# A new order inside each attention round: sums first, normalisation last, weight decoding from the fourth pair on

## The chip, the cores and the metric

The kernel runs on one core of one Trainium2 chip. The metric is the device time of one execution in microseconds (us); the time of a kernel is the median of its runs. Five engines work side by side, each through its own instruction stream in program order: PE (TensorE, matrix products; PEld is its loading of weights), DVE (VectorE), ACT (ScalarE), POOL (GpSimd) and SP (SyncE, which here only issues DMAs). They wait for one another through semaphores.

## The reference

Attention over 2 x 12 heads of 448 tokens and head size 64, with capped scores, then two gated layers. All arrays are float32 but the layers' weights, which arrive as float64.

```python
scores = cap * np.tanh(scale * (q @ k.T) / cap)
attn = np.exp(scores - max) ; attn = attn / (attn.sum(-1) + 1e-9)
x = (attn @ v)                                  # gathered to 896 tokens x 768
x = (silu(x @ w_gate) * (x @ w_val)) @ w_out    # 768 -> 1536 -> 768
x = (sigmoid(x @ w_gate2) * (x @ w_val2)) @ w_out2
```

## The kernel before, in words

Heads are handled in 12 pairs (b, p), two heads a pair, one pair a round of the loop over `i`. A float32 operand of a product is split into a high and a low part (`kh`, `kl`, `qh`, `ql`, `xh`, `xl`, `wh`, `wl`), and three products are summed. The schedule is written out by hand: each engine follows the order in which the program issues.

Keys come in three full blocks (c = 0 to 2) and a fourth, `NB`, in which both heads share a block. Round `i` does for pair `i`: `scores(i, c)` (PE into a two-bank PSUM tile `pss`, of which there are two, then a tanh on ACT into `e`), and `exponentials(i, part)` (exp on ACT, part 0 over blocks 0 and 1, part 1 over the rest). `sums(i, 0)` and `sums(i, 1)` (DVE) add the exponentials over blocks into `es`. One round later, `values(i - 1)` (PE) makes the numerators `pv` from `e` and `v` (16 products) and then the denominators `pd` from `es` and `e` (8 products). `taken_off` copies `pv` to `xu` and `pd` to `dn` and sends a row of `dn` for each head through a DMA into `g`. `inverted` takes the reciprocal of `g` (DVE), writes it to a DRAM tile `d`, and reads it back broadcast over partitions into `rb`. `normalized` multiplies `xu` by `rb` and splits the result into `xh` and `xl`, three operations on DVE.

`transposed(i + 2)` turns the next keys and queries on PE, and `qk_parts(i + 2)` splits them (four operations on DVE). `load` issues four DMAs a pair for k and q, `load_v` three for v. In the rounds, all DMAs are issued by SP, in program order: those of `load(i + 3)` and `load_v(i + 2)`, then `d` and two of `rb` in `inverted(i - 2)`, then `g` in `taken_off(i - 1)`.

`ws` is the stream of weights. A job loads 128 columns of a weight as 64-bit words (`r`, two buffers) and decodes them in four steps: L74 (DVE) and L75 (ACT); L77 and L78 (DVE); L80 (DVE) and L81 (ACT); L83 and L84 (DVE). A job that ends also issues the load of the job after next. Sixteen steps (four jobs) lie inside the attention, so that the first layer's products can start when the attention ends. After the rounds a written-out tail mixes the first products of the layer with the last pairs' values and normalisation; then the two gated layers run.

PSUM tiles of one bank (`pk`, `pq`, `pv`, `pd`) rotate through four buffers.

The edited functions and the loop follow, with the profile's line numbers.

Of the kernel before, what the change touches and what calls it, by code (L numbers as in the profile page):

```python
# [9 lines left out]
F32 = mybir.dt.float32  # L10
# [9 lines left out]
def attention_then_two_gated_layers(  # L20
# [14 lines left out]
    nc = tc.nc  # L35
    B, H, S, D = q.shape
    NT, DM = out.shape
    DFF = g1.shape[1]
    P = 128
# [3 lines left out]
    KD = DM // P  # L43
# [14 lines left out]
    xh = const.tile([P, KD, NT], F32R, tag="xh", name="xh")  # L58
    xl = const.tile([P, KD, NT], F32R, tag="xl", name="xl")
# [33 lines left out]
    class Stream:  # L93
# [11 lines left out]
        def load(self, upto):  # L105
            while self.loaded < min(upto, len(self.keys)):
                key = self.keys[self.loaded]
                src = self.jobs[key][0]
                r = wp.tile([P, src.shape[0] // P, src.shape[1]], I64, tag="r", name="r", bufs=2)
                nc.sync.dma_start(r, src.rearrange("(k p) f -> p k f", p=P))  # L110
                self.raw[key] = r
                self.loaded += 1
# [37 lines left out]
    def products(o, w, bh, bl, u, ks, nk, off=0):  # L150

        for kk in ks:
            for m, (a, x) in enumerate(((w[0], bh), (w[0], bl), (w[1], bh))):
                nc.tensor.matmul(  # L154
                    o,
                    lhsT=a[:, kk - off, :],
                    rhs=x[:, kk, halves[u]],
                    start=(kk == 0 and m == 0),
                    stop=(kk == nk - 1 and m == 2),
                )  # L160
# [133 lines left out]
    NPAIR = len(pairs)  # L294
    NB = S // P
    S0 = NB * P
    ws, pools, z_tiles = weights()
    with ExitStack() as actx:
        ap = actx.enter_context(tc.tile_pool(name="ap", bufs=2))
# [61 lines left out]
        def qk_parts(i, copy=nc.scalar.copy):  # L361

            pk, pq = turned.pop(i)
            kh, kl = [ap.tile([P, S0 + P], F32R, tag=n, name=n, bufs=2) for n in ("kh", "kl")]
            qh, ql = [ap.tile([P, S], F32R, tag=n, name=n, bufs=2) for n in ("qh", "ql")]
            nc.vector.tensor_copy(kh, pk)
            copy(qh, pq)
            nc.vector.tensor_tensor(kl, pk, kh.bitcast(F32), ALU.subtract)
            nc.vector.tensor_tensor(ql, pq, qh.bitcast(F32), ALU.subtract)
            operands[i] = (kh, kl, qh, ql)  # L370
# [3 lines left out]
        def scores(i, c):  # L374

            kh, kl, qh, ql = operands[i] if c < NB else operands.pop(i)
            if c == 0:
                ex[i] = ap.tile([P, 2 * NB + 1, S], F32, tag="e", name="e", bufs=2)
            keys = slice(c * P, (c + 1) * P)
            bank = bank2("pss")  # L380
            heads = rows if c < NB else [slice(0, P)]
            for t, (a, x) in enumerate(((kh, qh), (kl, qh), (kh, ql))):
                for j, r in enumerate(heads):
                    nc.tensor.matmul(bank[:, j, :S], lhsT=a[r, keys], rhs=x[r], start=(t == 0), stop=(t == 2))
            nc.scalar.activation(  # L385
                ex[i][:, 2 * c : 2 * c + len(heads)], bank[:, : len(heads), :S], AF.Tanh, scale=inv_sb
            )
# [7 lines left out]
        def sums(i, part):  # L395

            e = ex[i]
            if part == 0:
                es[i] = ap.tile([P, 2, S], F32, tag="es", name="es", bufs=2)
                nc.vector.tensor_tensor(es[i], e[:, 0:2], e[:, 2:4], ALU.add)  # L400
            else:
                nc.vector.tensor_tensor(es[i], es[i], e[:, 4:6], ALU.add)
# [3 lines left out]
        def values(i):  # L406

            e, tv, s = ex.pop(i), vt[i % NV], es.pop(i)
            pv, pd = bank1("pv"), bank1("pd")
            for c in range(NB + 1):  # L410
                for j in range(2):
                    y = e[:, 2 * c + (j if c < NB else 0)]
                    nc.tensor.matmul(pv[rows[j], :S], lhsT=tv[:, j, c, :], rhs=y, start=(c == 0), stop=(c == NB))
            for a, y in ((ones, s), (own, e[:, 2 * NB :])):
                for j in range(2):
                    nc.tensor.matmul(
                        pd[rows[j], :S], lhsT=a[:, j], rhs=y[:, j % y.shape[1]], start=(a is ones), stop=(a is own)
                    )
            nd[i] = (pv[:, :S], pd[:, :S])

        xu = {}
# [2 lines left out]

        def taken_off(i):
            n, d = nd.pop(i)
            xu[i] = ap.tile([P, S], F32, tag="xu", name="xu", bufs=3)
            dn = ap.tile([P, S], F32, tag="dn", name="dn", bufs=2)
            nc.scalar.copy(xu[i], n)
            nc.scalar.copy(dn, d)  # L430
            g = ap.tile([CP, 2 * R], F32, tag="g", name="g")
            nc.sync.dma_start(g, dn[0 : D + 1 : D])
            dens[i] = g

        def inverted(i):
            g = dens.pop(i)
            nc.vector.reciprocal(g, g)
            d = dr.tile([2 * S], F32, tag="d", name="d")
            nc.sync.dma_start(d.rearrange("(p c) -> p c", p=CP), g)
            rb[i] = ap.tile([P, S], F32, tag="rb", name="rb", bufs=2)  # L440
            for j in range(2):
                nc.sync.dma_start(rb[i][rows[j]], d[j * S : (j + 1) * S].unsqueeze(0).to_broadcast([D, S]))
# [7 lines left out]
        def normalized(i):  # L450
            b, p = pairs[i]
            x = ap.tile([P, S], F32, tag="x", name="x", bufs=2)
            nc.vector.tensor_tensor(x, xu.pop(i), rb.pop(i), ALU.mult)
            o = slice(b * S, (b + 1) * S)
            nc.vector.tensor_copy(xh[:, p, o], x)
            nc.vector.tensor_tensor(xl[:, p, o], x, xh[:, p, o].bitcast(F32), ALU.subtract)

        load(0, (nc.sync, nc.scalar))
        cap_sb = const.tile([P, 1], F32, name="cap_sb")
        nc.scalar.dma_start(cap_sb, cap.to_broadcast([P, 1]))  # L460
        wide_sb = const.tile([1, 1], mybir.dt.int32, name="wide_sb")
        inv_sb = fix.tile([P, 1], F32, name="inv_sb")
        near_sb = const.tile([P, 1], F32, name="near_sb")
        load(1)
        load_v(0)
        transposed(0)
        qk_parts(0)
        nc.vector.tensor_tensor(inv_sb, cap_sb, cap_sb, ALU.mult)
        nc.vector.tensor_scalar(wide_sb, inv_sb[:1], WIDEST**2, None, ALU.is_gt)
        nc.vector.tensor_scalar(near_sb, cap_sb, -WIDEST, WIDEST, ALU.max, ALU.min)  # L470
        nc.vector.reciprocal(inv_sb, near_sb)
        nc.vector.tensor_scalar_mul(inv_sb, inv_sb, scale)
        load(2)
        load_v(1)
        NS = 16
        for i in range(NPAIR):
            if i + 3 < NPAIR:
                load(i + 3)
            if i + 2 < NPAIR:
                load_v(i + 2)  # L480
            if i == 1:
                ws.load(2)
            if i > 1:
                inverted(i - 2)
            scores(i, 0)
            if i == 0:
                transposed(1)
                qk_parts(1, nc.vector.tensor_copy)
            scores(i, 1)
            exponentials(i, 0)  # L490
            if i > 0:
                sums(i - 1, 1)
                values(i - 1)
                taken_off(i - 1)
            for _ in range(NS * i // NPAIR, NS * (i + 1) // NPAIR):
                ws.step()
            sums(i, 0)
            scores(i, 2)
            scores(i, NB)
            exponentials(i, 1)  # L500
            if i + 2 < NPAIR:
                transposed(i + 2)
                qk_parts(i + 2, nc.vector.tensor_copy)
            if i > 1:
                normalized(i - 2)
        last = NPAIR - 1
        inverted(last - 1)
        sums(last, 1)
        ws.through(("v", 0, 0))
        begun = {0: (gate_banks(), value_banks())}  # L510
        w0 = [ws.take("g", 0, 0), ws.take("v", 0, 0)]
        products(begun[0][0][0], w0[0], xh, xl, 0, range(KD), KD)
        values(last)
        products(begun[0][1][0], w0[1], xh, xl, 0, range(KD), KD)
        normalized(last - 1)
        inverted_here(last)
        normalized(last)
        ws.through(("v", 0, 1))
        for o, w in zip(begun[0], w0):
            products(o[1], w, xh, xl, 1, range(KD - 1), KD)  # L520
        begun[1] = (gate_banks(), value_banks(), ws.take("g", 0, 1), ws.take("v", 0, 1))
        products(begun[1][0][0], begun[1][2], xh, xl, 0, range(KD), KD)
        for o, w in zip(begun[0], w0):
            products(o[1], w, xh, xl, 1, [KD - 1], KD)
    wide = nc.values_load(wide_sb[0:1, 0:1], min_val=0, max_val=1, skip_runtime_bounds_check_because="the result of a comparison")
    gated_layers(ws, pools, z_tiles, xh, xl, begun)

# [5 lines left out]
    with tc.If(wide != 0):  # L533
        xh = const.tile([P, KD, NT], F32R, tag="xh", name="xh_any")
# [95 lines left out]
```

## Time and profile before

| what | value |
|---|---|
| median of 3 runs | 667.99 us (666.84 to 668.14) |
| the profiled execution | 667.57 us |
| its span, first to last instruction | 665.8 us |
| PE, DVE, ACT busy | 96%, 68%, 42% of the span |
| values(0) starts | 26.35 us |
| values(10) starts | 117.35 us |
| layers' products start | 124.36 us |

The profile is of one execution. Times in its rows count from the span's first instruction; between the span and the time of the execution lie 1.8 us that no row shows. In the prediction V is the start of `values(i - 1)` in round i, and it serves as the mark of a round. The attention fills the first fifth of the span, and the gated layers the rest.

### The profile page before, as it was taken

The page shows a single profiled execution, that of the slowest core. Times are in us where ns is not written, and L with a number is a line of the kernel's source. Part 1 is how long each engine was busy: PE and PEld are TensorE (multiplying, and loading weights), DVE is VectorE, ACT ScalarE, POOL GpSimd, SP SyncE. Part 2 cuts the span into 40 slices and gives each one's busy share as a digit, 9 for nine tenths or more (in the row PEclk, how much of TensorE's full clock was granted, in tenths as well). Part 3 has the DMA queues.
Part 4 walks back from the last instruction along what each step waited for, and adds up shares of the span by engine and source line. Part 5 has one row for each costly group of instructions (what it writes and reads, how often), then busy time and mean ns, then how long its engine had stood idle before and what let it go on. Part 6 is the DMA issues. An engine that isn't in the chain of part 4 may idle for free. (4 is left out here: it accounts for less than half of the span.)

```text
span 665.8 us, 8385 instructions
## 1 busy us (share of the span) xinstructions
PE 642.1 (96%) x3311; PEld 546.6 (82%) x3311; DVE 453.6 (68%) x667; ACT 281.0 (42%) x363; POOL 3.3 (1%) x24
## 2 busy tenths in 40 slices
PE   6598999999999999999999999999999999999996
PEld 3354544499999999999999999999999999999995
DVE  3487787638879777997778667777787774694000
ACT  3598888604434433443334334334343332342000
POOL 2000000000000000000000000000000000000000
PEclk9699999999999999999999999999999999999998
DMA  5553542203434433433353423333443233161111
GB/s 140 148 146 94 137 115 85 76 1 95 138 100 142 143 96 95 143 114 123 117 168 100 139 95 95 114 124 103 135 137 101 95 98 94 58 206 43 41 29 33
DMA packets 99973, 70.86 MB, mean 106 GB/s; under 512 B 29142, under 2 KB 99926, under 8 KB 99926
## 3 DMA queue, kind: packets, MB, share of 16 engines
q1 hardware_dynamic: 98662, 69.80, 34.7%
q8 instruction: 28, 0.46, 0.3%
q10 hardware_dynamic: 1264, 0.45, 0.3%
q14 instruction: 19, 0.16, 0.1%
HBM read 67.40 MB, written 2.79 MB: 105 GB/s over the span
## 5 line engine op out<-in xcount | busy, mean ns | idle before, releaser
L75 ACT ACTIVATE c<-t,bias_sb 128x768 uint32<-128x768 uint32 x72 | 67.7, 940 | 94.3 <-DVE t L74 94.3
L81 ACT CAST wh<-c 128x768 fp32r<-128x768 f32 x60 | 50.4, 839 | 75.6 <-DVE c L80 75.6
L78 DVE SCALAR_TENSOR_TENSOR g<-r,g 128x768 f32<-128x768 uint32 x72 | 69.1, 959 | 2.5
L80 DVE SCALAR_TENSOR_TENSOR c<-r,c 128x768 uint32<-128x768 uint32 x72 | 68.5, 952 | 0.2 <-ACT c L75 0.2
L227 DVE TENSOR_TENSOR sg<-pv,sg 128x448 f32<-128x448 f32 x48 | 29.8, 620 | 51.0 <-PE pv L154 40.8
L84 DVE SCALAR_TENSOR_TENSOR wl<-g,t 128x768 fp32r<-128x768 f32 x60 | 57.5, 958 | 2.1
L228 ACT CAST hh<-sg 128x448 fp32r<-128x448 f32 x48 | 27.2, 567 | 73.6 <-DVE sg L227 73.6
L154 PE MATMUL pg<-xh,wh 128*128 128x448 f32 x144 | 52.8, 367 | 0.7 <-ACT e L385 0.7
L154 PE MATMUL pg<-hl,wh 128*128 128x448 f32 x144 | 53.0, 368 | 0.0
L154 PE MATMUL pg<-hh,wl 128*128 128x448 f32 x144 | 53.0, 368 | 0.0
L154 PE MATMUL pg<-hh,wh 128*128 128x448 f32 x144 | 53.0, 368 | 0.0
L154 PE MATMUL pv<-xh,wh 128*128 128x448 f32 x144 | 52.8, 367 | 0.0
L154 PE MATMUL pv<-yh,wl 128*128 128x448 f32 x144 | 52.7, 366 | 0.0
L154 PE MATMUL pg<-xl,wh 128*128 128x448 f32 x144 | 52.7, 366 | 0.0
L154 PE MATMUL pg<-yh,wh 128*128 128x448 f32 x144 | 52.7, 366 | 0.0
L154 PE MATMUL pg<-yl,wh 128*128 128x448 f32 x144 | 52.7, 366 | 0.0
L154 PE MATMUL pv<-xh,wl 128*128 128x448 f32 x144 | 52.7, 366 | 0.0
L154 PE MATMUL pg<-xh,wl 128*128 128x448 f32 x144 | 52.7, 366 | 0.0
L154 PE MATMUL pg<-yh,wl 128*128 128x448 f32 x144 | 52.7, 366 | 0.0
L154 PE MATMUL pv<-yl,wh 128*128 128x448 f32 x144 | 52.7, 366 | 0.0
L154 PE MATMUL pv<-xl,wh 128*128 128x448 f32 x144 | 52.7, 366 | 0.0
L154 PE MATMUL pv<-yh,wh 128*128 128x448 f32 x144 | 52.7, 366 | 0.0
(97 smaller groups left out, 1268.9 us busy)
## 6 DMA issues: line engine op xcount, KB each, us to landing
r<-in_moe_w_gate_dram SPq DMA_DIRECT2D x24, 768.0 KB, 4.3
r<-in_moe_w_val_dram SPq DMA_DIRECT2D x24, 768.0 KB, 4.5
r<-in_moe_w_out_dram SPq DMA_DIRECT2D x24, 768.0 KB, 4.1
tq<-in_q_dram SPq DMA_DIRECT2D x11, 224.0 KB, 3.9
rb<-d SPq DMA_DIRECT2D x22, 112.0 KB, 2.8
kt<-in_k_dram SPq DMA_DIRECT2D x12, 192.0 KB
vt<-in_v_dram SPq DMA_DIRECT2D x12, 192.0 KB, 3.3
out_dram<-ob SPq DMA_DIRECT2D x4, 140.0 KB
```

The costliest lines, as they stand in the source:

```text
L75: nc.scalar.activation(c, t, AF.Relu, bias=bias_sb, scale=4096.0)
L78: nc.vector.scalar_tensor_tensor(g, low, 2.0**-32, g.bitcast(U32), ALU.mult, ALU.add)
L80: nc.vector.scalar_tensor_tensor(c, top, 0x80000000, c, ALU.bitwise_and, ALU.bitwise_or)
L81: nc.scalar.copy(hi, c.bitcast(F32).rearrange("p (k f) -> p k f", k=r.shape[1]))
L84: nc.vector.scalar_tensor_tensor(lo, g.rearrange("p (k f) -> p k f", k=r.shape[1]), 2.0**-20, t.bitcast(F32).rearrange("p (k f) -> p k f", ...
L154: nc.tensor.matmul(o, lhsT=a[:, kk - off, :], rhs=x[:, kk, halves[u]], start=(kk == 0 and m == 0), stop=(kk == nk - 1 and m == 2),)
L227: nc.vector.tensor_tensor(sg, vs[u], sg, ALU.mult)
L228: nc.scalar.copy(hh[:, f, halves[u]], sg)
```

## The change

- In `taken_off`, `dn` is copied by DVE and no longer by ACT; `xu` has four buffers for three.
- In a round, DVE's order changes. Before: `inverted(i - 2)`, `sums(i - 1, 1)`, weight steps, `sums(i, 0)`, `qk_parts(i + 2)`, `normalized(i - 2)`. After: `sums(i - 1, 1)`, `inverted(i - 2)`, `normalized(i - 3)`, weight steps, `sums(i, 0)`, the copy of `dn`, `qk_parts(i + 2)`.
- ACT's weight steps go ahead of the copy of `xu` and not behind it.
- The sixteen weight steps are spread over rounds 3 to 11, and no longer over rounds 0 to 11. The first weight loads are those of `ws.load(2)` in round 1; before, the first step had loaded in round 0.
- `cap` is loaded through GpSimd's queue and no longer as ACT's third DMA, and the five small operations that make `inv_sb` and `near_sb` from it stand ahead of `qk_parts(0)`, no longer behind it.
- In the tail, `sums(last, 1)` goes ahead of `inverted(last - 1)`, the last pair is normalised ahead of the one before it, and of the six blocks of the contraction (one a pair of heads) the last two (from `KD - 2`) are multiplied behind another group of products, no longer only the last one.

```diff
-            xu[i] = ap.tile([P, S], F32, tag="xu", name="xu", bufs=3)
+            xu[i] = ap.tile([P, S], F32, tag="xu", name="xu", bufs=4)
-            nc.scalar.copy(dn, d)
+            nc.vector.tensor_copy(dn, d)
...
-        load(0, (nc.sync, nc.scalar))
-        nc.scalar.dma_start(cap_sb, cap.to_broadcast([P, 1]))
+        nc.gpsimd.dma_start(cap_sb, cap.to_broadcast([P, 1]))
+        load(0, (nc.sync, nc.scalar))
...
         transposed(0)
-        qk_parts(0)
         (five small operations: inv_sb, wide_sb, near_sb)
+        qk_parts(0)
...
+            if i > 0:
+                sums(i - 1, 1)
             if i > 1:
                 inverted(i - 2)
+            if i > 2:
+                normalized(i - 3)
             scores(i, 0)
...
             exponentials(i, 0)
             if i > 0:
-                sums(i - 1, 1)
                 values(i - 1)
-                taken_off(i - 1)
-            for _ in range(NS * i // NPAIR, NS * (i + 1) // NPAIR):
-                ws.step()
+            if i >= FIRST:                       # FIRST = 3
+                n = NPAIR - FIRST
+                for _ in range(NS * (i - FIRST) // n, NS * (i - FIRST + 1) // n):
+                    ws.step()
             sums(i, 0)
+            if i > 0:
+                taken_off(i - 1)
...
-            if i > 1:
-                normalized(i - 2)
         last = NPAIR - 1
+        sums(last, 1)
         inverted(last - 1)
-        sums(last, 1)
+        normalized(last - 2)
...
-        normalized(last - 1)
         inverted_here(last)
         normalized(last)
+        normalized(last - 1)
...
-            products(o[1], w, xh, xl, 1, range(KD - 1), KD)
+            products(o[1], w, xh, xl, 1, range(KD - 2), KD)
...
-            products(o[1], w, xh, xl, 1, [KD - 1], KD)
+            products(o[1], w, xh, xl, 1, range(KD - 2, KD), KD)
```

## Rows read from the trace of the kernel before

**Rows 1.** Busy time by stage: busy us of each engine (instructions), granted clock, DMA share

```profile
26.35:117.35 91.00, 86.48 (x524) 44.13 (x522) 69.60 (x111) 77.94 (x86) 0.00 (x0) 1.00 0.40 106
124.36:659.00 534.64, 534.64 (x2686) 491.20 (x2687) 367.38 (x526) 186.29 (x261) 0.00 (x0) 1.00 0.33 105
```

**Rows 2.** Timeline of rounds 0 and 1: start, us, engine, line, operation, [idle before]

```profile
21.34 0.56 DVE L74 TENSOR_SCALAR t<-r 128x768 uint32<-128x768 uint32 x1 [9.02 <-DMA r<-in_moe_w_gate_dram]
...
21.93 0.94 ACT L75 ACTIVATE c<-t,bias_sb 128x768 uint32<-128x768 uint32 x1 [7.95 <-DVE t L74]
22.77 1.51 ACT L385 ACTIVATE e<-pss,inv_sb 128x896 f32<-128x896 f32 x2
...
23.81 0.74 PE L384 MATMUL pss<-qh,kh 64*128 64x448 f32 x2 [9.89 <-ACT e L385]
...
26.35 3.54 PE L413 MATMUL pv<-e,vt 128*64 128x448 f32 x16
```

**Rows 3.** Timeline of PE: a round whose denominators wait for nothing, and the last V

```profile
33.77 0.47 PE L384 MATMUL pss<-qh,kh 64*128 64x448 f32 x2
...
35.17 3.23 PE L413 MATMUL pv<-e,vt 128*64 128x448 f32 x16
...
39.84 0.47 PE L384 MATMUL pss<-qh,kh 64*128 64x448 f32 x2
...
43.67 3.23 PE L413 MATMUL pv<-e,vt 128*64 128x448 f32 x16
...
117.35 3.23 PE L413 MATMUL pv<-e,vt 128*64 128x448 f32 x16
```

**Rows 4.** Timeline of DVE around the round with V at 62.57 us

```profile
60.87 0.69 DVE L366 CAST kh<-pk 128x512 fp32r<-128x512 f32 x1 [1.42 <-PE pk L356]
...
63.73 0.62 DVE L453 TENSOR_TENSOR x<-xu,rb 128x448 f32<-128x448 f32 x1 [0.51 <-DMA rb<-d]
...
65.48 1.04 DVE L402 TENSOR_TENSOR es<-es,e 128x896 f32<-128x896 f32 x1
66.43 0.95 DVE L80 SCALAR_TENSOR_TENSOR c<-r,c 128x768 uint32<-128x768 uint32 x1
67.42 0.56 DVE L83 TENSOR_SCALAR t<-c 128x768 uint32<-128x768 uint32 x1
...
68.89 1.08 DVE L400 TENSOR_TENSOR es<-e 128x896 f32<-128x896 f32 x1
```

**Rows 5.** Waits in the attention: who waited for whom, us in total, times, longest

```profile
PEld pd L416 <- DVE es L402: 10.4, 8, 2.1
```

**Rows 6.** Timeline of ACT, same round

```profile
62.51 1.89 ACT L385 ACTIVATE e<-pss,inv_sb 128x896 f32<-128x896 f32 x2
...
68.34 0.53 ACT L430 COPY dn<-pd 128x448 f32<-128x448 f32 x1 [1.70 <-PE pd L416]
68.77 0.84 ACT L81 CAST wh<-c 128x768 fp32r<-128x768 f32 x1
```

**Rows 7.** Timeline of SP's DMA issues: every g from the round with V at 52.59

```profile
61.54 0.57 SPq L432 DMA_DIRECT2D g<-dn  x1
...
70.17 0.58 SPq L432 DMA_DIRECT2D g<-dn  x1
...
80.58 0.57 SPq L432 DMA_DIRECT2D g<-dn  x1
```

**Rows 8.** Timeline of the start, before round 0's first tanh

```profile
4.33 0.34 POOL L328 MEMSET own<- 64x64 f32 x2
...
6.86 0.69 DVE L366 CAST kh<-pk 128x512 fp32r<-128x512 f32 x1 [5.69 <-PE pk L356]
...
8.73 0.15 DVE L468 TENSOR_TENSOR inv_sb<-cap_sb 128x1 f32<-128x1 f32 x1
...
9.60 1.01 ACT L385 ACTIVATE e<-pss,inv_sb 128x896 f32<-128x896 f32 x1 [1.82 <-DVE inv_sb L472]
```

**Rows 9.** DMA issues of the attention: count, size, median us from issue to landing

```profile
tq<-in_q_dram SPq DMA_DIRECT2D x11, 224.0 KB, 3.9
...
d<-g SPq DMA_DIRECT2D x11, 3.5 KB, 1.9
```

More of the change, by code (lines that the diff above doesn't have):

```diff
@@ L472, in attention_then_two_gated_layers @@
         nc.vector.tensor_scalar_mul(inv_sb, inv_sb, scale)
+        qk_parts(0)
         load(2)
         load_v(1)
-        NS = 16
+        NS, FIRST = 16, 3
         for i in range(NPAIR):
@@ L491, in attention_then_two_gated_layers @@
             if i > 0:
-                sums(i - 1, 1)
                 values(i - 1)
+            if i >= FIRST:
+                n = NPAIR - FIRST
+                for _ in range(NS * (i - FIRST) // n, NS * (i - FIRST + 1) // n):
+                    ws.step()
+            sums(i, 0)
+            if i > 0:
                 taken_off(i - 1)
-            for _ in range(NS * i // NPAIR, NS * (i + 1) // NPAIR):
-                ws.step()
-            sums(i, 0)
             scores(i, 2)
```

## The prediction, made before the changed kernel ran

> **What bounds the kernel now.** I read the busy time by stage first. From 124.36 us on PE is busy all the time and at the full clock [rows 1]: the gated layers are PE's, and what the attention saves arrives whole at the end, as long as the layers find their weights. The wait list names no wait of PE behind that point. The attention is another matter: in the 91.0 us between V of round 1 and V of round 11, ten rounds of 9.1, no engine is full [rows 1]. So I read timelines there, the start first.
>
> In round 0 the first decoding step stands in the middle of DVE's and ACT's order, and its weight has not landed: DVE waits 9.02 us for the DMA, ACT 7.95 for DVE, PE 9.89 for ACT's tanh [rows 2]. That is one chain, counted once. It also costs clock: before the wait products run at 0.47 us a pair, behind it at 0.74, and from the first product to V go 2.54 us where a later round takes 1.40 [rows 2, 3].
>
> In the steady rounds the round whose denominators wait for nothing takes 43.67 - 35.17 = 8.50 [rows 3]. PE issues its products in it without a gap that another engine makes, so I take 8.50 as PE's floor. The other rounds are longer because `pd` waits for the second sum, 10.4 us in 8 waits [rows 5]. That sum is late on DVE because it stands behind `normalized`, which itself waits for `rb` (0.51 us in the round shown) and then takes, with the reciprocal, 65.48 - 63.73 = 1.75 [rows 4].
>
> **Part 1, decoding from round 3.** The wait in round 0 goes. ACT is free at 21.93 - 7.95 = 13.98 and can start the tanh that it started at 22.77 [rows 2]: 8.79 us. With the idle time gone I expect the clock to stay up: 2.54 - 1.40 = 1.14 more [rows 2, 3]. Sum 9.9. What is late next is the first load of round 3's weights; issued in round 1, it has two rounds, about 17 us, to land. In before, the first weight was waited for 9 us. Nothing there.
>
> **Part 2, cap through GpSimd.** This is a loss. POOL first works through its memsets, to 4.33 + 0.34 = 4.67 us [rows 8]. No row shows a DMA issued by POOL. The nearest bounds are a small transfer, 1.9 us to landing, and one of the queries, 3.9 [rows 9]: cap is there between 6.57 and 8.57. The five small operations now stand in front of `kh`, which could start at 6.86. They take at most 9.60 - 8.73 = 0.87, and from `kh` to the first tanh go 9.60 - 6.86 = 2.74 [rows 8]. So the first tanh comes at landing + 3.61, 10.2 to 12.2 for 9.60: 0.6 to 2.6 lost. I take the middle, 1.6, as neither row is a POOL transfer. The start then gains 9.9 - 1.6 = 8.3, bounds 7.3 to 9.3.
>
> The Trainium skill speaks against this edit ("DMA: Bandwidth & Descriptors", section "Specifications"): a transfer that GpSimd issues has its first byte after about 1 us, one from SyncE or ScalarE after about 0.6 us, as software writes the descriptors. By the page's fixed cost of about 2.0 us ("Anatomy of one DMA") cap would land at an estimated 6.7, and the start would gain 9.2. No row here shows it.
>
> **Part 3, the second sum first.** PE's order in a round does not change. On DVE `qk_parts` ends at 63.73 - 0.51 = 63.22, 0.65 behind V at 62.57 [rows 4]. The sum follows at once, 0.95 [rows 4], ends by V + 1.6 and is wanted by `pd` about V + 3.1 (the eight product pairs of `pv` take most of 3.23 [rows 3]). So it has about 1.4 us to spare, and the waits of [rows 5] go. At most the ten rounds come down to 10 x 8.50 = 85.0: a gain of 6.0.
>
> **Part 4, what the new order takes back.** The copy of `dn` leaves ACT (0.53, behind a wait of 1.70 for `pd` [rows 6]) and comes to DVE; I price it there at the same 0.53. DVE's work in a round is then 2.35 for `qk_parts`, 0.95, 1.75, about 1.0 for the first sum, 0.53 for `dn`: 6.6. Decoding is 0.99 for L80, 1.47 for L83 and L84 [rows 4], and as much as L83 and L84 for L77 and L78, 0.59 for L74: 4.5 a job. Four jobs in nine rounds make 2.0 a round: 8.6 against PE's 8.50. DVE is just full, with the 1.4 to spare as its cushion: by itself nothing.
>
> The order has a price, though. In rounds 4 and 6 the steps are L77, L78, L80, L81. DVE reaches them at V + 0.65 + 0.95 + 1.75 = V + 3.35, ends L80 at 3.35 + 1.47 + 0.99 = 5.8; ACT's L81 (0.84 [rows 6]) and `xu` (about 0.5) run to V + 7.1. All of this is now in front of the tanh of block 2, whose products start at V + 39.84 - 35.17 = V + 4.67 and are done by V + 5.4 (two blocks take 1.40 [rows 3]). The tanh is thus 1.7 late. Its PSUM tile is wanted by the next round's first scores at V + 8.50 - 1.40 = V + 7.1, and it takes 0.95, half of a pair of tanhs [rows 6]: 0.75 of the delay is hidden, and about 0.9 stalls PE. In round 5 (L83, L84, L74, then L75 at 0.94 [rows 2]) the same sum gives 0.7. Later rounds have the ACT step near the front of DVE's work, or none: nothing. Together 2.5.
>
> SP is the other price. Between two issues of `g` lie 70.17 - 61.54 = 8.63, and 10.41 where a weight load goes out as well [rows 7]. The order of SP's DMAs in a round stays as it was: seven loads, `d`, a wait for `d` to land, two `rb`, `g`. At 8.50 a round SP is as full as PE, and two weight loads fall in rounds 5 and 7. Over eight rounds SP needs 6 x 8.63 + 2 x 10.41 = 72.6 where PE needs 68.0: 4.6 behind, of which the stalls above cover 2.5 and DVE's cushion 1.4. The rest, 0.7, I count; bounds 0 and all 3.5 that is left of the 6.0.
>
> So the rounds gain 6.0 - 2.5 - 0.7 = 2.8, bounds 0 and 6.0.
>
> **Part 5, the tail.** PE has no wait of a tenth of a us behind 124.36 [rows 1], with the old order too; the new one moves waits on DVE, where nothing of PE's is due. Nothing. If `normalized(10)` came late, two blocks of products are now behind 18 others, so the cover has grown.
>
> **The sum.** 8.3 + 2.8 = 11.1. The profiled execution took 667.57, 0.42 under the median of the runs; it would take 656.5, and the median 656.9.
>
> **Rivals.** First, SP or DVE paces the rounds as slowly as now (9.1): `normalized` is only about one sum and one reciprocal later than before, so `rb` may still hold DVE up, and now the decoding, the first sum, `dn`, and with `dn` the next `g` stand behind it. For it speaks that SP's gaps [rows 7] are as long as the rounds; against it, that the sum which PE waits for is ahead of it. Only the start gains: 668.0 - 8.3 = 659.7. Second, PE's floor holds in all rounds, DVE and ACT catching up in the light ones: 668.0 - 8.3 - 6.0 = 653.7, or 652.7 with cap at its early bound. Third, slower than before: the loop `rb`, `normalized`, `dn`, `g`, `d`, `rb` becomes longer than two rounds and feeds itself. V of round 1 would be at about 18.0; to eat that up the ten rounds must average (117.35 - 18.0) / 10 = 9.9. A round at the 10.41 of [rows 7] each time would end 4.8 later than before: 672.8. Only a weight load in every round would do that, and there are two or three. Fourth, the change does not do what it says: round 0's wait only moves, as round 1's queries, issued in the same full SP queue, come late. Then perhaps half of the start remains, 664. Their DMAs were issued before that first weight's, so I hold little of it.
>
> **Chances and range.** The forecast 0.58, SP or DVE as pace 0.20, PE's floor 0.16, the moved wait 0.03, slower 0.03. Faster by over 0.2% (1.3 us, about what a measurement of this kernel can tell from no change) 0.96, within it 0.01, slower 0.03. The range goes from both best bounds, 668.0 - 9.3 - 6.0 = 652.7, to the worst of the start with no gain in the rounds, 668.0 - 7.3 = 660.7.
>
> **What would show it.** V of round 1 near 18 and no wait of DVE for a weight's DMA; cap landing as the wait in front of L468; the clock full in the second slice; no wait of `pd` for the second sum; V to V 8.5 in rounds 1 to 3 and above 9 in rounds 4 to 6, with PE waiting for a tanh behind L81. The prediction is wrong if DVE waits for `rb` or `g` in most rounds, if cap takes longer than the queries did, or if PE finds work missing behind the attention.

## The result and the profile after

| | before | changed |
|---|---|---|
| median (runs) | 668.07 us (666.84 to 668.18, 4) | 658.91 us (658.4 to 660.1, 4) |
| ratio | | 0.987, 95% interval 0.9851 to 0.9888 |
| profiled execution, its span | 667.57, 665.8 | 659.29, 657.5 |
| V of round 1 | 26.35 | 19.91 |
| ten rounds, V of 1 to V of 11 | 91.0 | 89.60 |
| V of round 11 to the layers' first product | 7.01 | 6.63 |
| layers' first product | 124.36 | 116.14 |

The median came 2.0 us above the forecast of 656.9 and inside its range. The medians differ by 9.16 us and the profiled executions by 8.28, where 11.1 were forecast. The table says where: the start gained 26.35 - 19.91 = 6.44 (forecast 8.3), the rounds 1.40 (2.8), the stretch behind them 0.38 (0). All marks are of one execution of each kernel.

The timeline of the changed kernel's start stands against [rows 2, 8]:

```profile
8.02 0.16 DVE L467 TENSOR_TENSOR inv_sb<-cap_sb 128x1 f32<-128x1 f32 x1 [6.83 <-DMA cap_sb<-in_cap_dram]
...
8.72 0.68 DVE L366 CAST kh<-pk 128x512 fp32r<-128x512 f32 x1
9.55 0.74 PE L384 MATMUL pss<-qh,kh 64*128 64x448 f32 x2 [2.75 <-DVE kh L366]
...
11.50 1.01 ACT L385 ACTIVATE e<-pss,inv_sb 128x896 f32<-128x896 f32 x1 [4.12 <-PE pss L384]
...
14.71 1.01 ACT L385 ACTIVATE e<-pss,inv_sb 128x896 f32<-128x896 f32 x1 [2.20 <-PE pss L384]
...
19.91 3.23 PE L413 MATMUL pv<-e,vt 128*64 128x448 f32 x16
```

The wait for the weight is gone. DVE's first wait is now for `cap`, as forecast; the first tanh comes at 11.50, and landing + 3.61 would be 11.63. What was not forecast is the 0.74 behind PE's wait of 2.75 us: PE computes at half its clock (granted 0.50 from 9.5 to 13.5 us), and ACT waits another 2.20 us for the second block's scores. The one `cap` transfer, in the view of its tile:

```profile
L459 POOL DMA_DIRECT2D cap_sb<-in_cap_dram x1: 667/667/667, 4.6 to 4.6; - x1
...
DMA to landing us min/median/max: 3.4/3.4/3.4
```

The busy time by stretch of the changed kernel gives the granted clock, the third number from the end (0.83, 1.00, 0.91):

```profile
0.00:20.00 20.00, 15.07 (x70) 9.25 (x72) 7.70 (x18) 8.05 (x8) 3.95 (x25) 0.83 0.58 139
20.00:40.00 20.00, 20.00 (x124) 10.25 (x126) 13.42 (x22) 17.30 (x18) 0.00 (x0) 1.00 0.63 180
...
60.00:80.00 20.00, 17.64 (x102) 8.99 (x100) 17.93 (x29) 16.02 (x17) 0.00 (x0) 0.91 0.50 133
```

V to V, in us: 8.51, 8.50, 8.50 (rounds 1 to 3), 9.35, 9.14, 10.64, 9.91 (rounds 4 to 7), 8.51, 8.50, 8.04 (rounds 8 to 10). PE's timeline shows what stands in the four long ones:

```profile
53.36 0.47 PE L384 MATMUL pss<-qh,kh 64*128 64x448 f32 x2 [0.78 <-ACT e L385]
...
62.51 0.47 PE L384 MATMUL pss<-qh,kh 64*128 64x448 f32 x2 [0.57 <-ACT e L385]
...
72.88 0.47 PE L384 MATMUL pss<-qh,kh 64*128 64x448 f32 x2 [1.79 <-ACT e L385]
...
74.55 4.62 PE L413 MATMUL pv<-e,vt 128*64 128x448 f32 x16
...
84.46 3.23 PE L413 MATMUL pv<-e,vt 128*64 128x448 f32 x16
```

Rounds 4, 5 and 6 end in a wait of PE for a tanh. In round 4, whose V is at 45.42, ACT's timeline shows what the tanh stands behind:

```profile
51.13 0.84 ACT L81 CAST wh<-c 128x768 fp32r<-128x768 f32 x1 [2.04 <-DVE c L80]
...
52.30 1.53 ACT L385 ACTIVATE e<-pss,inv_sb 128x896 f32<-128x896 f32 x2
```

In round 5 L75 stands in L81's place. Round 7 has no wait; its `pv` takes 4.62 us where it takes 3.23 at full clock [rows 3], and that is its excess. The waits in the attention no longer name `pd` behind the second sum [rows 5]. A new one is there:

```profile
PE pss L384 <- ACT e L385: 3.4, 4, 1.8
...
DVE g L437 <- DMA g<-dn: 0.9, 1, 0.9
```

It lies in round 6. Here is its chain in the timeline, from SP's queue to ACT:

```profile
61.00 0.58 SPq L110 DMA_DIRECT2D r<-in_moe_w_gate_dram  x1
...
61.72 0.58 SPq L432 DMA_DIRECT2D g<-dn  x1
...
66.48 0.20 DVE L437 RECIPROCAL g<-g 112x8 f32<-112x8 f32 x1 [0.93 <-DMA g<-dn]
...
69.67 0.95 DVE L80 SCALAR_TENSOR_TENSOR c<-r,c 128x768 uint32<-128x768 uint32 x1
...
70.66 0.83 ACT L81 CAST wh<-c 128x768 fp32r<-128x768 f32 x1 [2.62 <-DVE c L80]
```

The next weight's load was issued by the step of round 5 that ends a job (weight steps now go ahead of `taken_off`), so it stands ahead of `g` in SP's order. `g`, a transfer of a few KB, is read 4.76 us behind its issue (66.48 - 61.72); the small transfer of [rows 9] lands in 1.9. DVE waits 0.93 for it, with all of the decoding behind it, ACT then waits 2.62 for L80, and PE 1.79 for the tanh behind L81.

### The profile page after: what moved, and what is told of

It reads as the page before. It is cut to its first block, busy times and chain, and to the rows that moved or that the text cites. A ratio compares the mean times of both kernels' runs of the same rounds, so it can differ in the third digit from the quotient of the medians.

```text
span 657.5 us, 8373 instructions
## 1 busy us (share of the span) xinstructions
PE 642.7 (98%) x3311; PEld 548.3 (83%) x3311; DVE 459.1 (70%) x678; ACT 276.0 (42%) x352; POOL 3.9 (1%) x25
## 5 line engine op out<-in xcount | busy, mean ns | idle before, releaser
L75 ACT ACTIVATE c<-t,bias_sb 128x768 uint32<-128x768 uint32 x72 | 67.7, 940 | 87.1 <-DVE t L74 87.1
L81 ACT CAST wh<-c 128x768 fp32r<-128x768 f32 x60 | 50.3, 839 | 81.2 <-DVE c L80 81.1
L78 DVE SCALAR_TENSOR_TENSOR g<-r,g 128x768 f32<-128x768 uint32 x72 | 69.0, 959 | 2.5
L80 DVE SCALAR_TENSOR_TENSOR c<-r,c 128x768 uint32<-128x768 uint32 x72 | 68.5, 951 | 0.8 <-ACT c L75 0.7
```

The source lines that it names most:

```text
L75: nc.scalar.activation(c, t, AF.Relu, bias=bias_sb, scale=4096.0)
L78: nc.vector.scalar_tensor_tensor(g, low, 2.0**-32, g.bitcast(U32), ALU.mult, ALU.add)
L80: nc.vector.scalar_tensor_tensor(c, top, 0x80000000, c, ALU.bitwise_and, ALU.bitwise_or)
L81: nc.scalar.copy(hi, c.bitcast(F32).rearrange("p (k f) -> p k f", k=r.shape[1]))
```

## The experiments

Times are ratios to the kernel before, run on the same chip, with 95% intervals; the changed kernel's own is 0.987 (0.9851 to 0.9888). Repeated runs of one kernel differ by 0.5 to 5 us, so most of these intervals touch, and the finer comparison is of marks, one execution each. Rounds are V to V, from round 1 on.

**The start.** First theory: the loss against the forecast is the clock, which fell in PE's wait for `kh`. Rival: the wait alone, from `cap`'s queue or from the place of the five small operations.

`cap` on ACT's queue again, behind ACT's two loads:

```diff
-        nc.gpsimd.dma_start(cap_sb, cap.to_broadcast([P, 1]))
         load(0, (nc.sync, nc.scalar))
+        nc.scalar.dma_start(cap_sb, cap.to_broadcast([P, 1]))
```

> The changed kernel with cap back on ACT's queue, third behind the first keys and queries; the five small operations stay ahead of the first split. Theory (the start lost 1.9 us because DVE waits for cap until 8.0 us, and about as much again because PE idles meanwhile and its clock falls to half): cap lands before the keys are turned, the first split starts near 6.9, no product of round 0 takes more than 0.5 us, and V of round 1 comes at 16.4 to 16.9 for 19.9; the median falls by about 3.3, to 655.6. Rival (round 0 is paced by the transfers that SP issues or by DVE's splits, cap only hides it): V of round 1 stays above 18.5 and the median above 657.5.

The ratio is 0.9846 (0.9812 to 0.988), with V of round 1 at 16.36 and the layers at 115.9; the median is 657.66, where the theory had 655.6. The timeline of its start:

```profile
6.18 0.16 DVE L467 TENSOR_TENSOR inv_sb<-cap_sb 128x1 f32<-128x1 f32 x1 [5.01 <-DMA cap_sb<-in_cap_dram]
...
7.71 0.47 PE L384 MATMUL pss<-qh,kh 64*128 64x448 f32 x2 [1.10 <-DVE kh L366]
...
11.17 1.01 ACT L385 ACTIVATE e<-pss,inv_sb 128x896 f32<-128x896 f32 x1 [0.78 <-PE pss L384]
```

PE waits 1.10 for 2.75, its products stay at 0.47, and round 1 begins 3.55 us earlier. Only 0.24 of that arrives at the layers: the ten rounds take 92.91 (8.52 8.51 8.5 11.73 9.94 10.88 9.76 8.5 8.5 8.07). Its waits tell why:

```profile
DVE g L437 <- DMA g<-dn: 6.9, 5, 2.9
...
PE pss L384 <- ACT e L385: 5.2, 3, 3.0
```

DVE now waits for `g` five times, 6.9 us in all. SP has issued DMAs one behind the other from its first us on, at a pace that the earlier start doesn't change (the fourth `g` goes out at 52.50, for 52.66 in the changed kernel), and the rounds run into it.

The five small operations behind `qk_parts(0)`, as before, with `cap` still through GpSimd:

```diff
         transposed(0)
+        qk_parts(0)
         (five small operations)
-        qk_parts(0)
```

> The changed kernel with the five small operations back behind the first split; cap still comes through GpSimd. Theory (it is the place on DVE that costs, not the queue): cap lands at 8.0 as now, but the split of the keys no longer waits for it; the first tanh starts near 9.6 as in the kernel before, V of round 1 at 16.4 to 17.0, the median near 655.7. Rival (the queue itself costs, for instance by delaying the other first transfers): V of round 1 stays above 18.5.

The ratio is 0.9873 (0.9841 to 0.9906), the median 658.77, where the theory had 655.7. V of round 1 is at 16.69 and the layers at 114.95; the rounds take 91.63, with 11.57 and 11.33 in rounds 4 and 6, and DVE again waits for `g`, 3.4 in all. The kernel with neither edit (below) has V of round 1 at 15.92. So each edit alone costs little: 0.44 for the new place on DVE (the run before) and at most 0.77 for GpSimd's queue. Of the 0.77 no wait for `cap` is seen: `kh` itself starts at 7.19, behind the transposed keys, for 6.45 in the kernel with neither edit and 6.86 in the kernel before, so the start varies by some 0.4 ahead of anything that an edit touches. Together the edits cost 19.91 - 15.92 = 3.99: only where DVE waits for a `cap` that comes through GpSimd does PE's clock fall.

Twelve empty products on PE between `transposed(0)` and the first scores, everything else as changed:

```diff
         transposed(0)
+        for _ in range(12):
+            nc.tensor.matmul(pw, lhsT=warm[:, :P], rhs=warm, start=True, stop=True)
```

> The changed kernel with 12 more empty products on PE between the first transposes and the first scores, so that PE is busy while DVE waits for cap. Theory: DVE still waits for cap until 8.0, but the granted clock stays at full, the products of round 0 take at most 0.5 us for 0.74, and V of round 1 comes near 18.0 for 19.9; the median falls by 1.5 to 1.9, to about 657.2. Rival (the delay of round 0 is all DVE's wait, and the low clock is hidden behind ACT): V of round 1 stays within 0.5 of 19.9 and the median within 0.5 of 658.9.

The ratio is 0.9847 (0.9813 to 0.988) and the median 657.17, as the theory had it; V of round 1 is at 18.05, the rounds take 89.25, and the layers start at 113.92. The timeline of PE and ACT:

```profile
9.54 0.47 PE L384 MATMUL pss<-qh,kh 64*128 64x448 f32 x2
...
12.84 1.01 ACT L385 ACTIVATE e<-pss,inv_sb 128x896 f32<-128x896 f32 x1 [0.78 <-PE pss L384]
```

The first product starts at the same time as in the changed kernel (9.54, 9.55) but takes 0.47 for 0.74: `cap` is as late as there, only PE's idle time is filled. So 19.91 - 18.05 = 1.86 us of the start is the clock, and the first theory holds for that part.

**The rounds.** Theory: rounds 4 and 5 are long by the order of the decoding, round 6 by `g` behind a weight load in SP's queue, round 7 by the clock that falls in round 6's wait. Rival: DVE or SP is simply full, and any edit only moves the loss.

Weight loads of the rounds held back until `g` is issued:

```diff
-                self.load(n + 3)
+                self.want = n + 3
+                if not self.hold:
+                    self.load(self.want)
...
+        ws.hold = True
         for i in range(NPAIR):
...
                 taken_off(i - 1)
+            ws.load(ws.want)
```

> The changed kernel, but a weight load that a step of the rounds would issue is held back until g is issued, so that on SP's queue g goes first and the 768 KB behind it, as in the kernel before. Theory (g lands late when a weight load is in front of it in the same queue, DVE's reciprocal waits for it, and with it the decoding, ACT and PE): DVE does not wait for g in round 6, PE waits there about 0.9 us for a tanh for 1.8, the clock stays full in round 7, and the ten rounds take 86.5 to 87.5 for 89.6; the median falls by about 2.5, to 656.4. Rival (SP is short of time whatever the order: the load then delays the next loads, d and rb by as much): DVE waits for g or rb a round later, and the median stays within 1 of 658.9.

The ratio is 0.982 (0.9793 to 0.9847), just clear of the changed kernel's, and the median 657.59. The rounds take 88.53, 1.0 above the theory's bound (8.5 8.5 8.5 9.37 9.13 9.36 8.52 8.51 9.51 8.63). SP and DVE in its timeline, around round 6:

```profile
61.83 0.58 SPq L435 DMA_DIRECT2D g<-dn  x1
62.46 0.45 SPq L111 DMA_DIRECT2D r<-in_moe_w_gate_dram  x1
...
65.58 0.20 DVE L440 RECIPROCAL g<-g 112x8 f32<-112x8 f32 x1
```

With `g` ahead of the load, DVE finds it there and waits for nothing. Round 6 falls from 10.64 to 9.36 and round 7 from 9.91 to 8.52: the wait and the clock that it cost. Rounds 4 and 5 stay. That is the theory's pattern; a wait of 1.5 for `g` comes back once, in round 9.

The three v loads of a round on GpSimd's queue, which takes 3 of some 12 DMAs from SP:

```diff
-                load_v(i + 2)
+                load_v(i + 2, nc.gpsimd)
```

> The changed kernel with the rounds' loads of v through GpSimd's queue and nothing else. Theory: the waits of the decoding order stay (rounds 4, 5 and 6 at 9.3, 9.1 and 9.3), but DVE does not wait for g in round 6 and the clock stays full in round 7; ten rounds 86.5 to 87.5 for 89.6, the layers' products at 113 to 114 for 116.1, the median 656 to 656.8. Rival (the long rounds 6 and 7 come from the decoding order alone): ten rounds within 0.7 of 89.6.

The ratio is 0.985 (0.9822 to 0.9877), the median 658.01. The rounds take 87.68 (8.51 8.5 8.5 9.41 9.23 9.42 8.51 8.5 8.5 8.6), and DVE waits 0.4 for `g`. The same two rounds mend by another means, which speaks for SP's queue as the cause. The layers start at 114.54, 1.60 earlier than in the changed kernel; the profiled execution is 1.08 shorter, as its end takes 2.2 us longer and its layers' products 1.7 less (last section).

Two weight steps a round in rounds 3 to 10, in place of sixteen over nine rounds:

```diff
-            if i >= FIRST:
-                n = NPAIR - FIRST
-                for _ in range(NS * (i - FIRST) // n, NS * (i - FIRST + 1) // n):
+            if FIRST <= i < FIRST + NS // 2:
+                for _ in range(2):
```

> The changed kernel with two weight steps in each of the rounds 3 to 10, so that a round has either steps 1 and 2 of a job or steps 3 and 4, and never steps 2 and 3 or 4 and 1; the work is the same. Theory (rounds 4 to 7 are long because ACT's decoding waits for DVE behind an earlier step, holds up the tanh, and the idle PE then loses its clock): no wait of PE for a tanh above 0.4 us in rounds 3 to 10, every V to V 8.4 to 8.6, the ten rounds 85 for 89.6; the median falls by 4 to 5, to about 654.4. Rival (SP's queue paces these rounds: g and rb late behind a weight load): rounds 4 to 8 still average 9 and more, DVE waits for g or rb, and the median stays above 657.

The ratio is 0.9927 (0.9902 to 0.9952): the kernel is slower than the changed one, as the rival had it. The rounds take 92.62 (8.51 8.5 8.5 8.5 10.22 8.73 11.58 9.8 9.53 8.75). Its timeline, SP and DVE:

```profile
52.81 0.53 SPq L110 DMA_DIRECT2D r<-in_moe_w_gate_dram  x1
53.44 0.57 SPq L432 DMA_DIRECT2D g<-dn  x1
...
58.06 0.20 DVE L437 RECIPROCAL g<-g 112x8 f32<-112x8 f32 x1 [2.09 <-DMA g<-dn]
```

Round 4's excess of 0.85 is gone (8.5), so it did come from which steps stand in the round. Both kernels have two there, the changed one the second and third of a job and this one the third and fourth; without L77 and L78 ahead of L80, ACT's L81 starts at 49.62 for 51.13. But a job now ends every second round, its load goes ahead of `g` each time, and DVE waits for `g` three times, 6.5 us together. A schedule that looks better on DVE is worse through SP.

Both together, two steps a round and weight loads behind `g`:

> Both: steps in pairs 1-2 and 3-4 over rounds 3 to 10, and weight loads behind g. Theory (both ACT's decoding behind a second DVE step and g behind a weight load stall PE, and each alone leaves the other): V to V 8.5 in all ten rounds, their sum 85 to 86, the median 654 to 655. Rival (SP's queue is full by itself): sums of the waits of DVE for g and rb above 2 us, the rounds 88 and more, median above 657.

The ratio is 0.9828 (0.9789 to 0.9868), the median 657.02. The rounds take 87.77, five of them 8.5 (8.51 8.5 8.5 8.5 8.5 9.03 8.64 9.33 9.54 8.72); DVE waits for `g` 1.3 in all. Rounds 4 and 5 are at the floor, so both causes are real and separate, but the 85 to 86 of the theory did not come. Rounds 6 to 10 still take up to 9.54: with two steps in a round DVE's work, by the terms of Part 4, is 6.6 + 4.5/2 = 8.85 us, more than PE's 8.50. In the trace DVE is busy 8.33, 8.54, 8.80 and 8.73 us of rounds 6 to 9, and its only waits from there to the last round are the 1.3 for `g` and 0.3 for `rb`.

`dn` copied by ACT again:

```diff
-            nc.vector.tensor_copy(dn, d)
+            nc.scalar.copy(dn, d)
```

> The changed kernel with the copy of dn back on ACT. The prediction priced dn's move at nothing by itself, as DVE has 1.4 us to spare. Theory: rounds 1 to 3 stay at 8.5; in rounds 4 to 6 ACT's copy of dn stands in front of the late tanh and adds 0.4 to 0.5 to each stall: ten rounds 90.5 to 92, the layers' products 1 to 2 later, the median 660 to 661. Rival (DVE is full and gains what dn took): ten rounds 88.5 or less, the median below 658.

The ratio is 0.9871 (0.9844 to 0.9899), not to be told from the changed kernel's. In the trace the rounds take 91.61 for 89.60, with 12.81 in round 6; the stretch behind the rounds takes 6.93 for 6.63. Its timeline in round 6:

```profile
68.31 0.20 DVE L437 RECIPROCAL g<-g 112x8 f32<-112x8 f32 x1 [1.80 <-DMA g<-dn]
...
72.50 0.83 ACT L81 CAST wh<-c 128x768 fp32r<-128x768 f32 x1 [3.50 <-DVE c L80]
...
73.66 0.54 ACT L430 COPY dn<-pd 128x448 f32<-128x448 f32 x1
74.08 1.55 ACT L385 ACTIVATE e<-pss,inv_sb 128x896 f32<-128x896 f32 x2
...
75.16 0.74 PE L384 MATMUL pss<-qh,kh 64*128 64x448 f32 x2 [3.11 <-ACT e L385]
```

On ACT the copy stands between a late L81 and the tanh that PE waits for, and the tanh is later by it (0.54); the wait for `g` ahead of it is longer too, 1.80 for 0.93. DVE's copy takes 0.62 but stands in front of no tanh.

**What the order is worth.** Only the first round of the decoding, on the kernel before; order, `dn`, `cap` and tail stay as they were:

```diff
-        NS = 16
+        NS, FIRST = 16, 3
...
+            if i >= FIRST:        # spread as in the change
```

> The kernel before with one line of the change: decoding steps from round 3 on, spread as in the changed kernel; order, dn and cap as before. Theory (the start brings most of it, 9.9 us with cap in its old place; the rounds stay as they were at 9.1 because the second sum is behind normalized): V of round 1 at 16.4, ten rounds 91 to 92, the median 657.5 to 658.5, so that order and dn together bring no more than cap's new place takes away. Rival (without the new order the rounds become longer, as SP is nearer to its limit): ten rounds 93 and more, median above 660.

The ratio is 0.9833 (0.9805 to 0.986), at least as good as that of the whole change. V of round 1 is at 15.92, the rounds take 91.18 (8.51 10.36 8.92 8.91 8.91 8.92 8.88 8.91 9.97 8.89), and the layers start at 114.1, which is 2.04 earlier than in the changed kernel. Its waits:

```profile
PEld pd L416 <- DVE es L402: 11.0, 9, 2.4
...
DVE x L453 <- DMA rb<-d: 3.2, 3, 1.5
DVE g L437 <- DMA g<-dn: 3.0, 1, 3.0
```

`pd` still waits for the second sum nine times, and a round still takes 8.9. So the rest of the change is worth 91.18 - 89.60 = 1.58 in the rounds and 0.37 behind them, and costs 3.99 at the start: these are the 2.04.

The same with the v loads on GpSimd's queue:

> The kernel before with decoding from round 3 on and, in the rounds, the loads of v through GpSimd's queue; the old order of a round stays. Theory (with SP relieved the new order shows its worth: in the old one the second sum waits behind normalized and each round takes 8.9): ten rounds 88.5 to 89.5, the layers' products near 112, and 3 to 4 later than in the run of the new order with all three and v on GpSimd. Rival (the sum was late only because rb was late through SP): V to V falls to 8.5 to 8.6 here as well, and the two orders differ by less than 1.5.

The ratio is 0.9814 (0.9784 to 0.9843). The rounds take 88.33 (8.51 8.5 8.94 8.98 8.82 9.0 8.85 8.93 8.9 8.9), `pd` waits 7.5 for the second sum, and the layers start at 111.35. With SP relieved, the old order runs at an even 8.9.

**A version faster than the changed kernel.** Two steps a round, weight loads behind `g`, and `cap` on ACT's queue:

> As the run with both, and cap on ACT's queue. Theory (the start's 3.5 us were lost again in the run with cap alone only because g stood behind weight loads): V of round 1 at 16.4, rounds 85 to 86.5, the median 650.7 to 652.5. Rival (SP's issue is the pace: its first loads run without a pause from 0.8 us on, so an earlier V only finds g, d and rb later): V of round 1 at 16.4, but V of round 8 within 1 us of that in the run with both alone, and the same median within 1 us.

The ratio is 0.9791 (0.9764 to 0.9819), the median 655.39. V of round 1 is at 15.99, but the rounds take 91.48 and DVE waits for `g` six times, 5.9 in all: once more the earlier start meets SP's pace. V of round 8 comes at 80.26, for 80.29 in the run with both alone, as the rival had it. With the v loads on GpSimd's queue on top:

> As the run with all three (pairs, weight loads behind g, cap on ACT's queue), and in the rounds the three loads of v go through GpSimd's queue, no longer SP's. The layers' products started at 114.1 there, with V of round 1 at 16.0 and 91.5 for ten rounds. Theory (SP's chain of issues and landings, some 8.6 us a round and 10 with a weight load, sets the rounds; an earlier start only makes DVE wait for g): three issues of about 0.6 less leave SP 6.7 a round, DVE's waits for g nearly vanish, V to V is 8.5 to 8.7, the ten rounds 85 to 87, the layers' products start at 108 to 110, the median 650 to 652. Rival (DVE, with 8.6 us of work a round, is itself the pace): the ten rounds stay above 89.5.

The median is 654.27, the ratio 0.9788 (0.9765 to 0.9812). Its interval lies wholly under the changed kernel's, but overlaps that of the one-line kernel, 0.9805 to 0.986. V of round 1 is at 16.82, the rounds take 87.77 (8.52 8.51 8.5 8.5 8.5 9.05 8.71 9.97 8.8 8.71), and the layers start at 111.22. The rounds did not come to 8.5 each, and neither the theory's 85 to 87 nor the rival's 89.5 was met. Busy time from V of round 1 to the layers in this kernel:

```profile
16.80:111.20 94.40, 90.91 (x557) 47.36 (x555) 82.61 (x132) 81.62 (x85) 14.23 (x24) 1.00 0.50 132
```

and in the old order with the same v loads:

```profile
16.02:111.35 95.33, 92.63 (x557) 46.61 (x555) 78.01 (x123) 86.60 (x96) 14.23 (x24) 1.00 0.47 126
```

DVE is busy 82.61 of 94.40 in the new order and 78.01 of 95.33 in the old; the layers start 0.13 apart. The layers were to start 3 to 4 us apart if the new order had its worth here. With the waits of SP's queue nearly gone, new order and old come out alike.

## Why the prediction came out as it did

**Part 1 (decoding from round 3): right.** Forecast 9.9; alone on the kernel before it brought 26.35 - 15.92 = 10.43. Of this 0.41 lies ahead of `kh` (6.45 for 6.86), where the edit changes nothing, so about 10.0 is its own.

**Part 2 (`cap`): right in kind, too small.** Forecast a loss of 1.6, bounds 0.6 to 2.6; measured 3.99 against the kernel with Part 1 alone, or about 3.6 without the same 0.41. The landing was inside its bounds (8.02 between 6.57 and 8.57) and the first tanh came 1.90 later than before (11.50 for 9.60), so the sum held as far as the first tanh, though in part by luck: at full clock, in the run with empty products, it came 3.20 behind `cap`'s first reading (11.05 - 7.85) and not 3.61, and in the changed kernel the slow products filled most of the difference. By the Trainium skill ("DMA: Bandwidth & Descriptors", section "Anatomy of one DMA"; fixed cost about 2.0 us) `cap` would have landed at an estimated 6.7; here it took 3.4 us from the issue, and the measurement decides. On ACT's queue, behind two loads, it took 3.9 from an issue at 2.3; so `cap` is late by its issue behind POOL's memsets, at 4.64, and not by a slower transfer. The mis-sized term is the clock: the step "with the idle time gone I expect the clock to stay up" took away one wait of PE and overlooked that Part 2 puts another in its place, 2.75 us before the first product. Filling it with empty products gave back 1.86, and the 2.13 that remain are the late `cap` with the 0.41 in them (the first product starts at 9.54 for 7.42).

**Part 3 (second sum first): right.** No wait of `pd` for that sum is left, and six rounds take 8.51 or less.

**Part 4: two terms right, one too small.** The decoding's stalls in rounds 4 and 5, forecast 0.9 and 0.7, came as 9.35 - 8.50 = 0.85 and 0.64, by the mechanism named, a tanh behind L81 or L75; with another spread of the steps round 4 went to 8.50. Round 6 lost 0.86 to it where SP's queue did not interfere (9.36), for 0.9 forecast. The term "SP is the other price ... the rest, 0.7, I count" is the one that failed. Rounds 6 and 7 together lost 2.14 + 1.41 = 3.55 in the changed kernel and 0.86 + 0.02 = 0.88 with `g` ahead of the load: SP's order cost 2.67, of it 1.41 by the clock in round 7. The prediction counted SP's time and took its order for unchanged ("The order of SP's DMAs in a round stays as it was"); in fact the weight steps had moved ahead of `taken_off`, and with them a weight load ahead of `g`. It counted the DMAs that a moved step issues by their number and not by their place. The last round, 8.04 for 8.50, gave 0.46 back: no keys or queries are left to transpose there, which the floor of ten equal rounds left out.

**Part 5 (tail): nearly right.** 0.38 gained for 0. With `dn` on ACT the stretch takes 6.93, so most of it (0.30) is that copy's; the written-out tail's own edits show no more than 0.08.

**The sum.** 10.43 - 3.99 + 1.40 + 0.38 = 8.22 of the 8.28. The rivals: PE's floor in all rounds did not come, nor the slower loop, nor a moved wait for a load in round 0. The first one, SP as the pace, was half there: it cost two rounds in the changed kernel, and it takes back nearly all of a gain at the start (3.55 gained, 0.24 kept). The start as a whole gained 6.44, under its lower bound of 7.3. That the time still fell inside the range is in part luck: the range's slow end counted no gain in the rounds, and they gave 1.40. The median is even nearer to the first rival's 659.7 than to the forecast; only the traces tell the two apart, by rounds at PE's floor and a start that gained less. The forecast's direction held because it stood on the start, and there the large term was right.

**What stays open.** That DVE's work holds rounds 6 to 10 at 8.6 to 9.5 in the kernels with two steps a round is argued from its sum and its busy time; no run took work from it. A `cap` on ACT's queue with the small operations behind `qk_parts(0)` in the new order was not tried, nor the v loads on a queue other than GpSimd's.

## What to carry to other kernels

When a step moves ahead of another, ask what it issues and what small transfer now stands behind that in the same queue: place counts, not only number. A wait that a change takes from TensorE is worth its clock as well, so look for the new wait that comes in its place before counting the clock as saved. And run the one-line part of a large change alone: here it gave as much as the whole.

## What the runs showed of the hardware that was not expected

**The clock behind a short wait.** From round 1 on, in the changed kernel and all experiments, PE waited nine times for 1.77 to 3.11 us. Eight of these waits were followed by products at the lower of its two levels, 1.2 GHz (in the changed kernel the 1.79 in round 6; with `cap` on ACT's queue 2.95 and 1.93, where the next `pv` took 4.66 and 4.49 for 3.23); the granted clock of about 5 us behind each of them is 0.64 to 0.68. The ninth, with the empty products in the start, was as long as the first and the clock stayed at 2.4 GHz; PE's timeline and the busy time in that run (the changed kernel's row of the same stretch has 0.91):

```profile
71.05 0.47 PE L384 MATMUL pss<-qh,kh 64*128 64x448 f32 x2 [1.80 <-ACT e L385]
...
72.48 3.23 PE L413 MATMUL pv<-e,vt 128*64 128x448 f32 x16
...
60.00:80.00 20.00, 17.63 (x112) 9.54 (x112) 17.42 (x29) 16.18 (x18) 0.00 (x0) 1.00 0.53 141
```

The waits of 1.64 and less in these rounds were followed by products at full speed. What set the one of 1.80 apart stays open.

**A small transfer behind a large one.** On SP's queue `g` was read 4.62 to 4.76 us behind its issue when a weight load stood ahead of it (58.06 - 53.44, 66.48 - 61.72), and was there by 3.75 (65.58 - 61.83, DVE being busy until then) when the load stood behind. The traces also hold the times of single packets, and these show when it moves. In the changed kernel the packets of the load issued at 61.00 run from 62.31 to 66.01, and those of the `g` issued at 61.72 from 64.88 to 65.89: they start 3.16 us behind the issue, when most of the load has passed. The `g` of round 7, again behind a load, starts 3.23 behind its issue, the other nine 1.19 to 1.31, and all eleven of the kernel before, where no load stands ahead, 1.19 to 1.39. What holds the packets back was not tested by itself.

**Two paces of the same products.** From the layers' first product to the end of the span the kernels take 541.4 to 541.6 us, but 539.7 to 539.8 in three of them (those of the next finding apart). The groups of instructions place it, with no wait of PE between; in the changed kernel:

```profile
L154 PE MATMUL pg<-hh,wh 128*128 128x448 f32 x144 | 53.0, 368 | 0.0
```

and with two steps a round and loads behind `g`:

```profile
L157 PE MATMUL pg<-hh,wh 128*128 128x448 f32 x144 | 52.6, 365 | 0.0
```

The three groups of these products (`hh` and `hl` by `wh` and `wl`) make 3 x (53.0 - 52.6) = 1.2 us of the 1.7. Which kernels get the 365 follows no edit here; the cause stays open.

**A longer end.** PE's last product, in the timeline of the changed kernel:

```profile
651.02 0.37 PE L263 MATMUL po<-zxh,hl 128*128 128x448 f32 x1
```

and in that of the last version above, with the v loads on GpSimd's queue:

```profile
646.10 0.37 PE L266 MATMUL po<-zxh,hl 128*128 128x448 f32 x1
```

From its end to the end of the span lie 657.5 - 651.39 = 6.1 us in the one and 654.7 - 646.47 = 8.2 in the other. All three kernels with v loads on GpSimd's queue have 8.2 to 8.4 there, the others 6.1 to 6.3. That the queue is the cause was not tested otherwise; if it is, those kernels have some 2.1 us more to gain.
